# Layer two of a fourth batch in seven half-size products, squares and sums spread over three engines, and all pieces in a new order

## The chip, the core and the metric

The kernel runs on one NeuronCore of a Trainium2 chip. Five engines work side by side, each through its own list of instructions in a fixed order, and they wait for one another by semaphores: PE (TensorE) multiplies matrices into the accumulators of PSUM; DVE (VectorE), ACT (ScalarE) and POOL (GpSimd) do elementwise work; SP issues the stores. POOL also issues the loads of the inputs, as instructions in its own list, so that a load stands in line behind whatever POOL computes. The metric is the time of one execution on the device in microseconds (us). The kernel before took 225.02 us (median of three runs, 224.21 to 225.16).

## The reference

```python
scores = scale * np.matmul(x, state.transpose(0, 1, 3, 2))     # x: (8, 8, 512, 64), state: (8, 8, 32, 64)
a = softmax of scores over the 32 states;      xread = np.matmul(a, state)
scores2 = scale * np.matmul(state, x.transpose(0, 1, 3, 2))
a2 = softmax of scores2 over the 512 tokens;   sread = np.matmul(a2, x)
x = concatenate([xread, sread], axis=2), heads joined          # 8 batches x (512 + 32) rows x 512
h = x @ w_in                                                   # w_in: 512 x 2048
r = np.maximum(h, 0.0)
g = s * (r * r) + b
return g @ w_out                                               # w_out: 2048 x 512, out: 4352 x 512
```

(The softmaxes are shortened here.) Two cross attentions with 32 states to a head, and behind them a two-layer net whose activation is the squared rectifier.

## The kernel before

All inputs are cast to float16 on the way in; sums are float32. The eight batches run one behind the other in a pipeline, in the order 0 to 7, and the 256 rows of `sread` of all batches come last (`sr`).

The work is cut into pieces, each a small function, and the list `ORDER` names them one after the other: `name.argument.argument...`, where the letters A, V and G as an argument say ACT, DVE and POOL. The loop at the end of the kernel calls each piece in that order, so `ORDER` fixes the order of every engine's instructions; there is no other scheduler. The pieces that the text speaks of:

- Loads, all issued by POOL: `win.j` (a quarter of `w_in`), `wout.q` (a quarter of `w_out`), `x.b` and `xn.b` (a batch's `x` in two layouts), `st` (the states). Batch 0's `x` comes as float32 in four parts through SP's queue (`xf`) and is cast by `castx`. Eight loads of POOL can be under way; the ninth waits for the first to land. From batch 3 on `x.b` begins with a tiny copy (`ahead`) that waits for an earlier batch's transpose.
- First softmax: `xT` transposes `x` (DVE), `T` multiplies it with the states (PE), then `U`, `mu`, `D`, `E1`, `z`, `At`, `A`: transpose, maximum, subtraction, exponential (ACT), sum, scaling, transpose. For batch 0 they are done in two halves. `keep` copies `T` for later use. The second softmax is `nm`, `nms`, `E2`, `a2`, `aps`, `a2T`, `V`, `srd`.
- Layer one: since `xread` is `a` times the states, `M.b.j` first multiplies the states of a batch with quarter `j` of `w_in` (PE), `Mc` casts the result, and `l.b.f` multiplies it with `A` for feature block `f` of 16: two matmuls 128x512, then the rectifier on ACT into a tile `r` that holds four blocks. `lh` is the same for half of batch 0's tokens and two blocks at once. The sums of `l` have two buffers of PSUM (`hps`), so the matmuls of a third `l` wait for the rectifier of the first.
- `s.b.f.n.engine` squares `n` blocks of `r` into the tile `g` (`sh` for the halves of batch 0, `ssr` for the last rows).
- Layer two, plain: `L.b.rr.q`, four matmuls 128x512 for 128 tokens and a quarter of the 16 blocks; after four of them `out.b.rr` scales, adds the bias and stores.
- Layer two, with seven products for eight (Strassen's scheme in Winograd's form): for batches 5, 6 and 7 and the last rows. `wsum` makes four sums of the weights (`w_T1` to `w_T4`), `S.b.k.h.engine` four sums of quarters of `g` (half `h` of each), `P.b.u` half a product: eight matmuls 128x256. `ev` adds a finished product into the output tile `osx`, `put` stores it. `S_sr`, `P_sr`, `ev_sr` are the same for the last rows.
- `idle.n` multiplies ones by ones `n` times into a tile that nobody reads.

Work of several batches is woven together: while layer two of one batch runs on PE, softmax and layer one of the next go on, and the line breaks in `ORDER` stand where a batch's layer one begins.

Of the kernel before, what the change touches and what calls it, by code (L numbers as in the profile page):

```python
# [11 lines left out]
FP16 = mybir.dt.float16  # L12
# [3 lines left out]
    "win.0 win.1 wout.0 x.1 win.2 wout.1 win.3 wout.2 wout.3 idle.11 castx.1.0.V castx.0.0.A xT.0.0.0 "  # L16
    "casts.A turn.0.4.A pair.0.4 xT.0.1.0 T.0.1.0 U.0.0 mu.0.0 sb castx.1.1.A castx.0.1.A D.0.V.0 "
    "xT.0.0.1 idle.6 xT.0.1.1 E1.0.0 T.0.0.1 keep.0.0 M.0.0.1 Mc.0.0.A z.0.0 At.0.V.0 A.0.0 idle.4 "
    "M.0.1.1 Mc.0.1.A lh.0.0.0 U.0.1 mu.0.1 D.0.V.1 lh.0.2.0 keep.0.1 sh.0.0.0.V sh.0.2.0.V E1.0.1 z.0.1 "
    "At.0.V.1 L.0.1.0 lh.0.6.0 sh.0.6.0.G L.0.0.0 M.1.0.1 Mc.1.0.A lh.0.4.0 A.0.1 lh.0.6.1 xT.1.0 "  # L20
    "sh.0.4.0.G xT.1.1 T.1.1 U.1 lh.0.0.1 lh.0.4.1 lh.0.2.1 sh.0.2.1.G mu.1 M.0.2.0 Mc.0.2.A L.0.0.1 x.2 "
    "L.0.1.1 st D.1.V sh.0.6.1.V keep.1 l.0.9 l.0.8 M.0.3.1 Mc.0.3.V l.0.10 s.0.8.2.V cps.0 cps.1 E1.1 "
    "l.0.13 z.1 l.0.11 s.0.10.2.V At.1.V M.1.1.1 l.0.12 Mc.1.1.A l.0.14 l.0.15 L.0.0.2 s.0.12.2.A M.1.2.1 "
    "A.1 s.0.14.2.V Mc.1.2.A cps.2 cps.3 c L.0.1.2 l.1.1",
    "l.1.0 sh.0.0.1.V xT.2 M.1.3.1 x.3 L.0.0.3 bias out.0.0 l.1.2 Mc.1.3.V l.1.3 L.0.1.3 out.0.1 L.0.2.0 "
    "pair.4.16 sh.0.4.1.G turn.4.12.A L.0.2.1 l.1.4 turn.12.16.V T.2.1 keep.2 s.1.0.4.V l.1.5 l.1.6 "
    "L.0.2.2 l.1.8 U.2 mu.2 l.1.7 L.0.2.3 out.0.2 D.2.V l.1.9 s.1.8.2.V l.1.15 M.2.1.0 E1.2 z.2 M.2.0.1 "
# [24 lines left out]
    "L.4.3.0 L.4.3.1 l.5.11 xT.7 a2T.0.V s.5.8.4.V M.6.1.0 Mc.6.1.A A.6 M.6.2.1 out.4.2 l.5.13 l.5.12 "
    "s.5.12.2.V L.4.3.2 l.5.15 l.5.14 s.5.14.2.V L.4.3.3 P.5.0 out.4.3 Mc.6.2.A l.6.1 P.5.1 T.7.1 "
    "S.5.2.0.V S.5.3.1.V S.5.1.1.V V.6.0 srd.6 U.7 P.5.2 l.6.2 ev.5.X1 S.5.2.1.V",
    "l.6.0 keep.7 P.5.3 l.6.3 mu.7 S.5.4.0.V l.6.5 P.5.4 l.6.7 ev.5.Y srd.0 l.6.4 P.5.5 P.5.6 D.7.V E1.7 "
    "l.6.8 S.5.4.1.V P.5.7 l.6.6 M.6.3.0 s.6.0.4.V M.7.0.1 ev.5.X2 z.7 l.6.9 P.5.8 ev.5.W1 P.5.10 At.7.V "
    "Mc.7.0.A Mc.6.3.A s.6.4.2.V l.6.10 xn.7 P.5.9 s.6.6.2.V A.7 l.6.12 ev.5.X3 M.7.1.0 Mc.7.1.V M.7.2.1 "
    "nm.7 l.6.13 P.5.11 l.6.11 ev.5.W2 put.5.0.0 put.5.0.1 l.6.14 P.5.12 l.7.2 s.6.8.4.V S.6.3.0.V "
    "S.6.1.0.V P.5.13 Mc.7.2.A l.6.15 ev.5.X4",
    "l.7.0 s.6.14.2.V s.6.12.2.V S.6.3.1.V M.7.3.1 P.6.0 l.7.1 Mc.7.3.A l.7.6 P.6.1 put.5.1.0 nms.7.V "  # L60
    "E2.7.0 P.6.2 ev.6.X1 S.6.2.0.V S.6.1.1.V S.6.2.1.V put.5.1.1 l.7.12 l.7.3 E2.7.1 s.7.0.4.V P.6.3 "
    "a2.7 P.6.4 P.6.5 l.7.11 l.7.5 ev.6.Y aps.7 l.7.4 a2T.7.V S.6.4.0.V nm.1 nms.1.V P.6.6 l.7.8 ev.6.X2 "
    "l.7.15 V.7 srd.7 l.7.7 P.6.7 E2.1.1 E2.1.0 xn.1 P.6.8 P.6.9 ev.6.W1 a2.1 l.7.10 l.7.9 s.7.8.4.A "
    "S.6.4.1.V aps.1 s.7.4.4.V a2T.1.V ev.6.X3 P.6.10 P.6.11 ev.6.W2 put.6.0.0 put.6.0.1 l.7.14 "
    "s.7.14.2.V V.1 srd.1 S.7.3.0.V l.7.13 P.6.12 s.7.12.2.V P.6.13 P.7.0 lsr.6 S.7.1.0.V ev.6.X4 "
    "put.6.1.0 lsr.1 P.7.1 S.7.3.1.V S.7.2.0.V lsr.5 P.7.2 S.7.4.0.V P.7.3 lsr.2 lsr.3 ev.7.X1 P.7.4 "
    "ev.7.Y",
    "lsr.0 S.7.1.1.V S.7.2.1.V P.7.6 P.7.5 ssr.0.2.V lsr.9 ev.7.X2 ssr.2.2.V lsr.7 P.7.7 ev.7.W1 "
    "put.6.1.1 S.7.4.1.V lsr.8 ssr.8.2.V P.7.8 ssr.6.2.V lsr.4 ssr.4.2.V S_sr.3.0.V S_sr.1.0.V lsr.14 "
# [9 lines left out]
def kernel(  # L79
# [369 lines left out]
    def layer1(tag, f, terms, ntok):  # L449
# [4 lines left out]
        if (tag, q) not in R_t:  # L454
            R_t[tag, q] = rpool.tile([P, 4, ntok], FP16, name=f"r_{tag}_{q}", tag="r")
# [95 lines left out]
    def block(b, i, j):  # L551

        return G_t[b][:, j::2, HALF * i : HALF * i + HALF]
# [193 lines left out]
```

## Time and profile before

The profiled execution took 224.36 us, of which 222.2 us are the span from the first to the last instruction; 2.2 us lie around it. The median of the three runs is 0.66 us above the profiled execution.

| engine | busy us | share of the span | instructions |
|---|---|---|---|
| PE, matmuls | 210.7 | 95% | 1816 |
| DVE | 183.6 | 83% | 267 |
| ACT | 141.8 | 64% | 243 |
| POOL | 43.4 | 20% | 73 |

A busy PE says only that a matmul is in flight: matmuls are pipelined, and one of 128x512 shows 379 ns while the next starts 216 ns after it. What PE can do is read from the distance of the starts. Idle time of an engine that isn't the bound costs nothing by itself.

### The profile page before, as it was taken

How to read it: one execution, taken by the hardware profiler on the slowest of the kernel's cores; microseconds unless marked ns; L12 is line 12 of the kernel's file. 1: busy time of each engine (PE TensorE's matmuls, PEld its weight loads, DVE VectorE, ACT ScalarE, POOL GpSimd, SP SyncE). 2: the span in 40 equal slices, each digit the busy share in tenths (PEclk: the TensorE clock that was granted, in tenths of full speed). 3: DMA queues.
4: the chain of work that ended last, by engine and by line, in shares of the span. 5: the costliest groups of instructions: out<-in, count | busy, mean ns of one | idle time of the engine just before them, and what ended most of it. 6: DMA issues, size and time to landing. Idle time of an engine off the chain costs nothing.

```text
span 222.2 us, 4473 instructions
## 1 busy us (share of the span) xinstructions
PE 210.7 (95%) x1816; PEld 115.8 (52%) x1816; DVE 183.6 (83%) x267; ACT 141.8 (64%) x243; POOL 43.4 (20%) x73
## 2 busy tenths in 40 slices
PE   6469999999999999999999999999999999999992
PEld 2234334444444443444454544457766778888881
DVE  1597998889769997989796799889999997966772
ACT  2475895776488869855787479485877858533400
POOL 8245504000273400046002160005200000000000
PEclk9999999999999999999999999999999999999999
DMA  6999993420557892048927397226903500440066
GB/s 158 227 207 206 205 193 58 101 72 20 100 112 117 112 174 50 16 100 120 192 47 133 96 128 124 49 45 101 141 2 65 127 0 3 94 99 0 3 134 149
DMA packets 23416, 22.67 MB, mean 102 GB/s; under 512 B 4196, under 2 KB 16996, under 8 KB 23396
## 3 DMA queue, kind: packets, MB, share of 16 engines
q0 software_dynamic: 16560, 12.26, 38.6%
q1 hardware_dynamic: 6160, 9.97, 18.2%
q8 instruction: 14, 0.23, 0.4%
q10 hardware_dynamic: 676, 0.16, 0.3%
q14 instruction: 6, 0.05, 0.1%
HBM read 25.72 MB, written 8.91 MB: 156 GB/s over the span
## 4 chain that ended last, share of the span: by engine, by line
PE 88%; DMA 4%; DVE 3%; ACT 3%; SPq 1%; issue 0%
PE ops L496 31%; PE hps L452 24%; PE opf_X L137 9%; PE opf_W L137 5%; PE mps L137 4%; DMA xf<-in_x_dram 4%; PE hps_sr L452 3%; PE opf_Y L137 2%; PE vps L137 2%; PE T_None L137 2%; PE aps L137 2%; PE ops_sr_X L137 2%; ACT M L152 1%; DVE xT L289 1%; PE ops_sr_W L137 1%; ACT rh L482 1%
## 5 line engine op out<-in xcount | busy, mean ns | idle before, releaser
L456 ACT ACTIVATE r<-hps 128x512 f16<-128x512 f32 x120 | 69.3, 610 | 29.8 <-PE hps L452 28.4
L496 PE MATMUL ops<-w_out,g 128*128 128x512 f16 x320 | 78.1, 379 | 1.3 <-DVE g L462 1.3
L452 PE MATMUL hps<-A,M 128*128 128x512 f16 x240 | 65.3, 380 | 0.5 <-DVE M L152 0.3
L496 PEld LDWEIGHTS <-g 128*128 128x128 f16 x320 | 30.3, 98 | 38.4 <-issue 2.8
L462 DVE TENSOR_TENSOR g<-r 128x1024 f16<-128x1024 f16 (+1 forms) x39 | 34.5, 897 | 8.1 <-ACT r L456 8.0
L452 PEld LDWEIGHTS <-M 128*128 128x128 f16 x240 | 21.9, 98 | 25.8 <-issue 4.7
L137 PEld LDWEIGHTS <-g 128*128 128x128 f16 x288 | 28.0, 98 | 6.4 <-issue 0.2
L152 ACT CAST M<-mps 128x1024 f16<-128x1024 f32 x28 | 28.0, 1013 | 1.8 <-PE mps L137 1.8
L192 POOL DMA_DIRECT2D xn<-in_x_dram x32 | 18.5, 588 | 29.2 <-PE vps L137 28.3
L506 DVE SCALAR_TENSOR_TENSOR osb<-ops,sb_bc,bias_bc 128x512 f32<-128x512 f32 x20 | 14.7, 734 | 1.0 <-PE ops L496 1.0
L180 POOL COPY ahead<-xT 1x2 f16<-1x2 f16 x5 | 1.8, 367 | 67.0 <-DVE xT L289 67.0
L456 ACT ACTIVATE r_sr<-hps_sr 128x256 f16<-128x256 f32 x16 | 6.2, 385 | 12.8 <-PE hps_sr L452 12.4
L564 DVE TENSOR_TENSOR g<-g 128x1024 f16<-128x1024 f16 x18 | 12.2, 685 | 2.0 <-PE opf_Y L137 1.9
L289 DVE STREAM_TRANSPOSE xT<-xh 128x1024 f32<-128x1024 f32 (+2 forms) x12 | 10.3, 871 | 3.2 <-ACT xh L152 3.2
L333 DVE TENSOR_REDUCE z<-E 128x32 f32<-128x1024 f16 (+1 forms) x9 | 9.9, 1095 | 3.7 <-ACT E L328 3.7
L137 PE MATMUL opf_X<-w_T,g 128*128 128x256 f16 x96 | 11.9, 273 | 0.0
L137 PE MATMUL mps<-w_in,stT 64*32 64x512 f16 x256 | 11.2, 383 | 0.2 <-ACT M L152 0.2
L318 DVE TENSOR_REDUCE mu<-U 128x32 f32<-128x1024 f32 (+1 forms) x9 | 9.9, 1097 | 0.2
L376 ACT ACTIVATE E<-T_None,nms 128x512 f16<-128x512 f32 x8 | 5.5, 691 | 6.9 <-DVE nms L372 4.4
L328 ACT ACTIVATE E<-Dm 128x1024 f16<-128x1024 f32 (+1 forms) x9 | 8.7, 963 | 1.8 <-DVE Dm L322 1.5
L322 DVE TENSOR_TENSOR Dm<-U,mu 128x1024 f32<-128x1024 f32 (+1 forms) x8 | 9.6, 1201 | 0.2
L314 DVE STREAM_TRANSPOSE U<-T_None 128x1024 f32<-128x1024 f32 x7 | 8.7, 1247 | 1.2 <-PE T_None L137 0.8
(94 smaller groups left out, 259.4 us busy)
## 6 DMA issues: line engine op xcount, KB each, us to landing
out_dram<-osb SPq DMA_DIRECT2D x32, 128.0 KB, 2.7
xn<-in_x_dram POOLq DMA_DIRECT2D x32, 128.0 KB, 5.7
xh<-in_x_dram POOLq DMA_DIRECT2D x14, 256.0 KB, 5.2
out_dram<-osx SPq DMA_DIRECT2D x24, 128.0 KB, 2.4
w_in<-in_moe_w_in_dram POOLq DMA_DIRECT2D x8, 256.0 KB, 10.6
w_out<-in_moe_w_out_dram POOLq DMA_DIRECT2D x4, 512.0 KB, 12.7
xf<-in_x_dram SPq DMA_DIRECT2D x4, 256.0 KB, 7.5
out_dram<-osb SPq DMA_DIRECT2D x4, 256.0 KB
```

The costliest lines, as they stand in the source:

```text
L137: return nc.tensor.matmul(out, lhsT, rhs, start=start, stop=stop, tile_position=tp, is_transpose=is_transpose, skip_group_check=skip,)
L152: (engine.copy if engine is nc.scalar else engine.tensor_copy)(out, in_)
L192: nc.gpsimd.dma_start(out=xn_t[b][32 * jh : 32 * jh + 32].rearrange("t h c d -> t h (c d)"), in_=x[b].rearrange("h (t jh c) d -> jh t h (c ...
L289: nc.vector.transpose(part(out, p, g), part(in_, p, g))
L318: nc.vector.tensor_reduce(part(mu, p), blk(part(at[b]["U"], p)), AX.X, ALU.max)
L333: nc.vector.tensor_reduce(part(z, p), blk(part(at[b]["E1"], p)), AX.X, ALU.add)
L452: nc.tensor.matmul(hps, lhsT, rhs, start=(i == 0), stop=(i == len(terms) - 1))
L456: nc.scalar.activation(R_t[tag, q][:, i], hps, AF.Relu)
L462: e.tensor_mul(g, r, r)
L496: nc.tensor.matmul(ops_t[tag, rr], G_t[tag][:, f, P * rr : P * rr + P], w_out_f(f), start=(f == 0), stop=(f == NKF - 1),)
L506: nc.vector.scalar_tensor_tensor(osb, ops_t.pop((tag, rr)), s_bc, bias_bc, ALU.mult, ALU.add)
L564: e.tensor_tensor(out, x, y, op)
```

## The change

Batch 4 joins the batches whose layer two is done in seven products: its 16 pieces `L` and 4 pieces `out` go, and 14 `P`, 4 sums `S` in five pieces and 7 `ev`, 4 `put` come. Squares, sums, subtractions (`D`), scalings (`At`), casts (`Mc`) and copies are dealt anew to DVE, ACT and POOL; sums can now be made in one piece instead of two halves (the 2 in the place of `h`). The tiles of `r` are taken in turn from three buffers with names of their own instead of from one pool of three (four for the halves). And `ORDER` is new throughout; of 21 idle matmuls three are left.

Pieces by engine, before and after:

| piece | before | after |
|---|---|---|
| squares `s` of two blocks | 23 DVE, 1 ACT | 11 DVE, 14 ACT, 13 POOL |
| squares `s` of four blocks | 16 DVE, 2 ACT | 9 DVE, 2 ACT |
| squares `sh` | 4 DVE, 4 POOL | 4 DVE, 4 POOL |
| squares `ssr` | 8 DVE | 3 DVE, 5 ACT |
| `S`, half | 24 DVE | 17 DVE, 7 POOL |
| `S`, whole | none | 3 DVE, 1 POOL |
| `S_sr` | 8 halves DVE | 4 halves DVE, 2 halves and 1 whole POOL |
| `wsum` | 8 halves DVE | 2 halves and 1 whole DVE, 2 halves and 1 whole POOL |
| `D`, full batch | 6 DVE, 1 POOL | 3 DVE, 4 POOL |
| `At`, full batch | 7 DVE | 4 DVE, 3 POOL |
| `Mc` | 4 DVE, 28 ACT | 11 DVE, 21 ACT |
| `a2T` | 4 DVE, 4 ACT | 1 DVE, 7 ACT |
| `nms` | 6 DVE, 2 ACT | 2 DVE, 6 ACT |
| `castx`, `casts` | 1 DVE, 4 ACT | 3 DVE, 2 ACT |
| `L` and `out` | 80 and 20 | 64 and 16 |
| `P`, `ev`, `put` | 42, 21, 12 | 56, 28, 16 |
| matmuls of `idle` | 21 | 3 |

```diff
-    "win.0 win.1 wout.0 x.1 win.2 wout.1 win.3 wout.2 wout.3 idle.11 castx.1.0.V castx.0.0.A xT.0.0.0 "
-    "casts.A turn.0.4.A pair.0.4 xT.0.1.0 T.0.1.0 U.0.0 mu.0.0 sb castx.1.1.A castx.0.1.A D.0.V.0 "
-    "xT.0.0.1 idle.6 xT.0.1.1 E1.0.0 T.0.0.1 keep.0.0 M.0.0.1 Mc.0.0.A z.0.0 At.0.V.0 A.0.0 idle.4 "
-    "M.0.1.1 Mc.0.1.A lh.0.0.0 U.0.1 mu.0.1 D.0.V.1 lh.0.2.0 keep.0.1 sh.0.0.0.V sh.0.2.0.V E1.0.1 z.0.1 "
...
+    "castx.1.0.V castx.0.0.A win.0 xT.0.1.0 casts.V idle.1 idle.1 turn.0.4.A pair.0.4 xT.0.0.0 T.0.1.0 "
+    "keep.0.0 win.1 win.2 U.0.0 mu.0.0 D.0.V.0 castx.1.1.A E1.0.0 M.0.0.1 z.0.0 castx.0.1.V xT.0.0.1 "
+    "xT.0.1.1 wout.0 sb x.1 Mc.0.0.A wout.1 T.0.0.1 At.0.V.0 A.0.0 keep.0.1 M.0.1.1 Mc.0.1.A lh.0.0.0 "
+    "M.1.0.0 U.0.1 mu.0.1 D.0.V.1 E1.0.1 lh.0.6.0 lh.0.2.0 Mc.1.0.V sh.0.0.0.V M.0.2.0 win.3 sh.0.6.0.G "
+    "z.0.1 sh.0.2.0.V At.0.V.1 A.0.1 Mc.0.2.A idle.1 lh.0.4.0 M.1.1.1 M.1.2.0 sh.0.4.0.V Mc.1.1.A L.0.0.0 "
+    "wout.2 l.0.8 st l.0.9 s.0.8.2.G xT.1.0 l.0.11 xT.1.1 T.1.1 keep.1 U.1 mu.1 lh.0.6.1 sh.0.6.1.G D.1.V "
+    "lh.0.4.1 Mc.1.2.A L.0.1.0 lh.0.2.1 lh.0.0.1 sh.0.0.1.G L.0.1.1 E1.1 M.0.3.0 Mc.0.3.V M.1.3.1 l.0.10 "
+    "s.0.10.2.A L.0.0.1 Mc.1.3.A l.0.14 z.1 l.0.15 L.0.1.2 wout.3 At.1.V L.0.0.2 pair.4.16 turn.4.12.V "
+    "A.1 l.0.12 sh.0.4.1.G l.0.13 cps.0 cps.1 s.0.12.2.A cps.2 cps.3 s.0.14.2.V c sh.0.2.1.V l.1.3 x.2 "
...
+    "P.5.9 At.7.G ev.5.X3 Mc.7.1.A l.6.9 put.4.1.0 P.5.10 l.6.5 P.5.11 ev.5.W2 nms.1.A E2.1.1 l.6.15 A.7 "
+    "l.6.13 P.5.12 s.6.12.2.V s.6.4.2.G P.5.13 put.4.1.1 P.6.0 put.5.0.0 s.6.8.2.A s.6.14.2.V S.6.3.0.V "
+    "S.6.3.1.V l.7.6 l.7.12 ev.5.X4 xn.7 S.6.1.2.V aps.7 P.6.1 a2T.7.V",
+    "l.7.0 l.7.15 P.6.2 l.7.7 l.7.5 V.7 srd.7 l.7.14 P.6.3 ev.6.X1 l.7.4 E2.1.0 l.7.3 S.6.2.2.G P.6.4 "
...
+    turns = {}
+
+    def in_turn(shape, name, tag, n):
+        k = turns[tag] = turns.get(tag, -1) + 1
+        return rpool.tile(shape, FP16, name=name, tag=f"{tag}{k % n}", bufs=1)
+
     def layer1(tag, f, terms, ntok):
...
-            R_t[tag, q] = rpool.tile([P, 4, ntok], FP16, name=f"r_{tag}_{q}", tag="r")
+            R_t[tag, q] = in_turn([P, 4, ntok], f"r_{tag}_{q}", "r", 3)
...
-        r = R_t[b, f, p] = rpool.tile([P, 2, HALF], FP16, name=f"rh_{b}_{f}_{p}", tag="rh", bufs=4)
+        r = R_t[b, f, p] = in_turn([P, 2, HALF], f"rh_{b}_{f}_{p}", "rh", 4)
...
+    HALVES = (slice(0, 4), slice(4, 8), slice(0, 8))
...
-        A = lambda i, j: block(b, i, j)[:, 4 * h : 4 * h + 4]
+        sl = HALVES[h]
+        A = lambda i, j: block(b, i, j)[:, sl]
...
-        out, x, y = (t[:, 4 * h : 4 * h + 4] for t in (S_sr(name), x, y))
+        out, x, y = (t[:, HALVES[h]] for t in (S_sr(name), x, y))
```

`weight_sum` takes its slices from `HALVES` in the same way.

## The prediction

> **What bounds the kernel now.** I read the table of stages first (busy time of each engine in stretches of the span), then the timeline, then the groups by form, then the page's rows of the DMA engines.
>
> ```profile
> core 0: us, PE busy (x) PEld busy (x) DVE busy (x) ACT busy (x) POOL busy (x), PEclk, DMA share, GB/s
> 0.00:14.00 14.00, 8.89 (x73) 3.39 (x73) 7.03 (x15) 5.99 (x10) 7.86 (x16) 1.00 0.98 195
> 14.00:26.00 12.00, 10.19 (x91) 5.14 (x84) 10.59 (x15) 9.11 (x14) 5.47 (x7) 1.00 1.22 206
> ...
> 40.00:80.00 40.00, 40.00 (x278) 16.96 (x277) 34.66 (x45) 28.81 (x47) 10.05 (x15) 1.00 0.50 92
> ...
> 160.00:200.00 40.00, 40.00 (x404) 29.64 (x403) 34.97 (x55) 25.49 (x46) 0.00 (x0) 1.00 0.28 58
> ```
>
> PE is busy without a hole from 40 us on. Whether it is really full, the starts tell:
>
> ```profile
> 59.26 1.46 PE L496 MATMUL ops<-w_out,g 128*128 128x512 f16 x6
> 60.55 0.59 PE L452 MATMUL hps<-A,M 128*128 128x512 f16 x2
> 60.98 1.24 PE L496 MATMUL ops<-w_out,g 128*128 128x512 f16 x5
> ```
>
> ```profile
> 153.29 1.03 PE L452 MATMUL hps<-A,M 128*128 128x512 f16 x4
> 154.15 1.04 PE L137 MATMUL opf_Y<-w_out,g 128*128 128x256 f16 x8
> 155.03 1.03 PE L452 MATMUL hps<-A,M 128*128 128x512 f16 x4
> ```
>
> Two matmuls 128x512 take 0.43 us from start to start (60.55 to 60.98), four 0.86 (153.29 to 154.15), eight of 128x256 0.88 (154.15 to 155.03; 0.87 where no other form precedes). All pieces of a kind keep these distances from 40 us to the end. So with `L` at 0.863, `l` 0.432, `P` 0.873, `lh` and `lsr` 0.436, `M` 0.43, and the small rest the same way, matmul work is 203.8 us, and the last matmul ends at 218.1. What PE loses lies at the start: by 37.12 us, when two late `L` of batch 0 begin, 21.3 us of work are done, so 15.9 us are lost, 12.0 of them before the first `lh` at 14.16. Behind the last matmul stand 4.0 us of eviction and store, the same in both kernels.
>
> **Part by part.**
>
> *The product.* 16 `L` at 0.863 are 13.8 us, 14 `P` at 0.873 are 12.2. All of it lies on PE, the path: -1.6 us. Nothing else in PE's work changes but the idle matmuls: the first eleven (1.46 to 5.2 us) and the next ten stand in holes where PE waits anyway (the transposed `xT` at 11.5, `Mc` at 13.7), so taking them out gives nothing by itself.
>
> *The engines.* By the means of the groups, DVE sheds squares (7 of 1.21 us, 12 of 0.68, 5 of 0.42), 3 `D` of 1.2, 3 `At` of 1.29, 7 half sums of 0.69, `S_sr`, `wsum`, `a2T`, `nms` and 4 evictions of 0.73, together 45 us, and takes 7 casts of 1.21, 7 evictions of 0.74, four whole sums of 1.21 and two small casts, 19 to 20: from 183.6 to about 159 us. ACT takes 13 squares of 1.08, 5 `ssr` (0.55 each, half of that row), 3 `a2T` of 1.02, and sheds 7 casts of 1.01: 142 to about 154. POOL: nearest rows are the 128x512 square of 1.06 us and the 128x1024 `D` of 1.91. That is 1.9 to 2.1 us for 1024 elements and about 4.1 for 2048; 13 squares, 7 halves and one whole `S`, 4 pieces' worth of `wsum`, 4 `D`, 3 `At`, `S_sr` and the four `sh` make 77 us, where it was 6. With its loads POOL stands at about 114 us. None of the three comes near PE's 202, so by sums PE stays the bound. In the loads of 4 us stretches along the new order one is over: ACT has about 6 us against 3.5 of PE's around `V.6.0`, `E1.7` and `s.6.2.2.A`; four `P` follow there, which need no rectifier. I take 0 for it; without that cover it costs up to 2.
>
> *What runs against POOL.* The trace has it twice:
>
> ```profile
> 24.16 1.04 POOL L462 TENSOR_TENSOR g<-rh 128x512 f16<-128x512 f16 x1 [2.24 <-ACT rh L482]
> 24.17 2.11 DVE L322 TENSOR_TENSOR Dm<-U,mu 128x1024 f32<-128x1024 f32 x1
> ...
> 70.36 1.27 DVE L343 TENSOR_TENSOR At<-E,rz 128x1024 f16<-128x1024 f16 x1
> 70.50 1.14 POOL L180 COPY ahead<-xT 1x2 f16<-1x2 f16 x1 [4.02 <-DVE xT L289]
> ```
>
> The `D` that starts with POOL's square takes 2.11 us where the other five average 1.22: it waits until POOL is done. POOL's tiny copy, 0.17 us otherwise, starts under DVE's `At` and ends with it at 71.63. DVE's transposes and reductions beside POOL's squares show no such wait (0.67 and 0.71 at 19 to 20 us). So an operation of DVE that reads two tensors of SBUF and an operation of POOL exclude each other. The Trainium skill says so too (SBUF — State Buffer, section "SBUF: two separate sides"): the pair of ports is locked for a whole instruction and the loser blocks fully; the trace agrees with 1.04 against 0.89 us of delay. In the new kernel some 65 such DVE operations stand against 71 us of POOL's new work in 205: a third begin while POOL works and lose half an operation, 1.1 us, about 25 us in all. DVE is then at 184, as full as now, and PE was packed with that. How much reaches PE is bounded below by 0 and above by the places with little room. Squares on POOL are mostly due 5 to 26 us of PE's work after their rectifier. The tightest chain: `l.6.5`, `s.6.4.2.G`, the four loads `xn.7`, `S.6.2.2.G`, `P.6.4`. From the end of `l.6.5` to `P.6.4` PE has 11.9 us of other work; rectifier 0.9, square 2.1, four loads of 0.59 and the whole sum 4.1 make 9.5. 2.4 are spare; behind the square, `P.6.0` has 0.5, and at the end `P_sr.5` behind `S_sr.4.2.G` 0.7. I take +0.3, ends 0 and +3.
>
> *The start.* Here the order of loads decides: 204 to 206 GB/s are moved without a pause until 33 us, so 512 KB take 2.5 us. POOL's waits give the landings now: `w_in` quarter 0 at 10.9, quarter 1 at 13.1, `w_out` quarter 0 at 15.6, and on at that pace. In the new order `w_in` quarter 2 lands at 15.6, `w_out` 0 at 18.1, `x.1` at 20.6, `w_out` 1 at 23.1, `w_in` 3 at 25.6, `w_out` 2 at 28.1. `w_out` 3 stands in POOL's list behind the squares `s.0.8.2.G`, `sh.0.6.1.G` and `sh.0.0.1.G`; the last is done near 28, so it lands near 33, where it landed near 31. PE's loss must be at least landing minus work done before: 13.6 for `M.0.3`, 13.1 for `L.0.1.2`, 14.6 for `cps.3`. The softmax chain of batch 0 gives the same: `E1.0.0` no longer stands behind the cast of the last `xf` (10.36), so `A.0.0` ends at 13.6 instead of 14.1, but `M.0.1` still waits for 13.1. `lh.0.0.0` starts at 13.6 to 13.9, and following DVE's list by the same rows `A.0.1` ends at 20.0 and `T.1.1` starts at 21.9, with 7.8 us of work done: 14.0 lost, where it was 13.8. Later the rectifiers cost some 0.7 now and may again. Bounds for the loss: 14.6 and 16.2 against 15.9. I take -0.1, the middle leaning up for the clock:
>
> ```profile
> 1.46 3.88 PE L660 MATMUL dps<-ones 128*128 128x512 f16 x11 [1.46 <-DVE ones L221]
> ...
> 3.14 0.15 PEld L660 LDWEIGHTS <-ones 128*128 128x128 f16 x1 [0.28 <-issue]
> 3.57 0.15 PEld L660 LDWEIGHTS <-ones 128*128 128x128 f16 x1 [0.28 <-issue]
> 4.00 0.15 PEld L660 LDWEIGHTS <-ones 128*128 128x128 f16 x1 [0.28 <-issue]
> ```
>
> The idle matmuls start 0.43 us apart until 4.2 us and 0.216 after: PE runs at half speed until 2.7 us of dense work have passed, though the rows give the clock as 1.00 throughout. The new kernel has two there, so PE will be slow until `M.0.1` and the `lh` make it dense, from 13.1 to some 16 to 19 us. Then `T`, `M` and three `lh` take twice as long; on the chain to `lh.0.4.0` that is about +0.8, half of which `w_out` 3 hides. The Trainium skill (TensorE: Matmul & The Clock Gate, section "Part 1: The HAM clock gate") asks for a busy window of about 3.4 us that doesn't start with the kernel; by it the full clock comes between 16.5 and 20 us, an estimate, and the sum would be 0.3 us higher.
>
> *The sum.* -1.6 (products) -0.1 (start) +0.3 (POOL) = -1.4. The profiled execution before is 224.36, so this one would be 223.0; on the median, 0.66 higher, 225.02 - 1.4 = 223.6 us.
>
> **Rivals.**
>
> 1. The start gains. If the clock is up early and `w_out` 3 is in time, the loss falls to 14.6: -1.3 instead of -0.1, and no wait on POOL: 222.1 to 222.5. For it: more work of layer one is ready before `w_out` is. Against: DVE's chain to `A.0.1` isn't shorter.
> 2. Slower: POOL's pace. If POOL's operations with their waits take twice the nearest rows (4.2 for 1024, 8.3 for 2048), the chain to `P.6.4` takes 15.8 instead of 9.5 against 11.9 of other work: PE waits 3.9 us, 1.6 of it already at `P.6.0`: 225.02 - 1.7 + 3.9 = 227.2. It is slower by over 0.5% from a delay of 2.8 us on, POOL at about 1.8 times the rows; at 1.5 times (1 to 1.5 us at PE) it is about even. For it: five operations of POOL with two inputs are all that the trace shows. Against: the four squares took 1.04 to 1.10.
> 3. Slower: the clock stays down. If PE stays slow until 26 us, the 12 us from 14 on yield half: 6 us less work, less some 2.5 of waiting that there is anyway: +3.5, so 226.8. For it: PE has about 2 us of work in the 12 us before. Against: now it stays up through a hole of 2.1 us (before the `T` at 11.51).
> 4. The work saved doesn't show: small waits at PE of 1.6 us in all eat it: 225.0.
>
> **How the numbers follow.** A measurement of this kernel can tell about 0.5% from no change, 1.1 us: faster is under 223.9, slower over 226.1. Chances: forecast 0.45 (its own range 222.9 to 224.6, 0.31 of it under 223.9), start gains 0.15, POOL's pace 0.18 (0.13 slower, 0.05 even), clock 0.10 slower, nothing shows 0.12 (0.03 slower). Faster 0.31 + 0.15 = 0.46, same 0.14 + 0.05 + 0.09 = 0.28, slower 0.13 + 0.10 + 0.03 = 0.26. The range reaches from the first rival's end, 222.0, to just under the prices of the second and third, 227.0.
>
> **What would show it.** Right: `P` and `L` still 0.87 and 0.86 apart from 40 us on; 112 more matmuls of `opf` and 64 fewer of `ops`; DVE near 160 plus what it is blocked; the last matmul some 4 us before the end. The start is read from the work done by 37 us. Wrong if PE shows holes behind 40 us that `S` or squares on POOL end (step of POOL), if a 128x1024 square on POOL is far from 2.1 us, or if `hph` starts stay 0.22 apart beyond 20 us (clock).

## The result and the profile after

The changed kernel takes 241.27 us (median of four, 240.07 to 241.38), the kernel before on the same chip 225.09 (four, 224.21 to 225.94). The ratio is 1.071, with a 95% interval of 1.065 to 1.076: some 16 us slower, where 223.6 was forecast and 222.0 to 227.0 was the range. The profiled execution took 240.07 us with a span of 238.3, against 222.2 before.

The page of the changed kernel, its first rows: busy time by engine, then PE and its granted clock in 40 slices of 6 us.

```profile
PE 209.8 (88%) x1846; PEld 121.2 (51%) x1846; DVE 177.6 (75%) x229; ACT 154.1 (65%) x259; POOL 112.6 (47%) x106
PE   1489989799937999999999995599999989999992
PEclk9999999999997999999999999799999999999998
```

The sums are near the forecast ones: ACT was put at 154 us, POOL at 114, DVE at 159 plus what it is held. The row of PE shows what isn't: two holes, at about 66 to 71 and 143 to 155 us, and a dip of the clock behind each. The table of stages says the same (the columns are as in the table before):

```profile
0.00:14.00 14.00, 4.92 (x54) 1.65 (x54) 7.44 (x17) 5.34 (x9) 7.97 (x16) 1.00 0.98 195
14.00:26.00 12.00, 11.57 (x105) 5.64 (x98) 9.68 (x16) 10.53 (x17) 5.85 (x5) 1.00 1.22 207
40.00:80.00 40.00, 32.88 (x236) 14.01 (x221) 34.17 (x31) 23.16 (x38) 27.87 (x26) 0.96 0.61 106
80.00:120.00 40.00, 40.00 (x341) 17.95 (x340) 31.75 (x41) 31.13 (x55) 17.47 (x17) 1.00 0.44 80
120.00:160.00 40.00, 34.70 (x295) 20.11 (x294) 34.68 (x37) 25.12 (x46) 18.00 (x17) 0.96 0.42 67
160.00:200.00 40.00, 38.91 (x418) 27.75 (x417) 28.95 (x43) 30.58 (x50) 18.87 (x14) 1.00 0.43 80
```

From 40 to 80 us PE stands idle for 7.1 of 40, where it had no hole before; from 120 to 160 for 5.3. In the first of these POOL works 27.9 us instead of 10.1. From 80 to 120 us PE has no hole, and in the first 40 us it is busy 3.4 us less than before, with 18 idle matmuls gone.

The timeline at the first hole. Each row is one instruction or group: start, length, engine, line, operation, tiles, and in brackets the idle time before it and what ended that.

```profile
61.79 3.82 DVE L386 TENSOR_SCALAR a<-E,q 128x512 f16<-128x512 f16 x1
63.26 2.14 POOL L543 TENSOR_TENSOR w_T<-w_out 128x1024 f16<-128x1024 f16 x1
65.53 3.83 DVE L386 TENSOR_SCALAR a<-E,q 128x512 f16<-128x512 f16 x1
67.32 1.88 POOL L469 TENSOR_TENSOR g<-r 128x1024 f16<-128x1024 f16 x1
71.88 0.69 ACT L377 ACTIVATE E<-T_None,nms 128x512 f16<-128x512 f32 x1 [6.00 <-DVE U L315]
73.19 1.01 PE L459 MATMUL hps<-A,M 128*128 128x512 f16 x2 [5.47 <-ACT r L463]
```

The two scalings `a2.3` take 3.82 and 3.83 us; the same operation took 0.35 us in the kernel before, where the groups give the usual lengths of a scaling and of a square (busy time in all, then the mean in ns):

```profile
L385 DVE TENSOR_SCALAR a<-E,q 128x512 f16<-128x512 f16 x16 | 4.9, 350 | 0.4
L462 DVE TENSOR_TENSOR g<-r 128x1024 f16<-128x1024 f16 x23 | 15.2, 677 | 6.0 <-ACT r L456 6.0
```

The first scaling ends with POOL's half sum `wsum.T3.0.G` (63.26 to 65.40), the second with the two squares `s.2.0.2.G` and `s.2.2.2.G` behind it (65.35 to 69.20). Behind the scalings DVE has `nm.4` and `U.4`; ACT stands 6.00 us at `E2.4`, which by the profile waits for `U.4` (both read the same sums), and behind `E2.4` stand the rectifiers that PE waits 5.47 us for. The second hole:

```profile
143.27 2.34 POOL L193 DMA_DIRECT2D xn<-in_x_dram  x4
143.80 6.44 DVE L469 TENSOR_TENSOR g<-r 128x1024 f16<-128x1024 f16 x1
145.62 4.06 POOL L543 TENSOR_TENSOR w_T<-w_out,w_T 128x2048 f16<-128x2048 f16 x1
150.94 0.60 ACT L463 ACTIVATE r<-hps 128x512 f16<-128x512 f32 x1 [5.53 <-DVE g L469]
151.58 1.01 PE L459 MATMUL hps<-A,M 128*128 128x512 f16 x2 [5.30 <-ACT r L463]
```

A square of 0.68 us takes 6.44 and ends 0.56 us after POOL's whole sum `wsum.T4.2.G`. It holds the tile `r` that the next rectifier wants. These three instructions make 12.7 of the 13.9 us by which DVE's operations exceed their usual lengths in the whole kernel.

The clock, in stretches around the first hole (the number behind that of POOL is the granted clock):

```profile
68.00:72.60 4.60, 0.00 (x0) 0.00 (x0) 4.53 (x5) 0.72 (x3) 3.52 (x5) 1.00 0.65 84
72.60:76.00 3.40, 2.81 (x13) 1.55 (x13) 3.37 (x6) 2.53 (x5) 0.00 (x0) 0.50 0.86 134
76.00:80.00 4.00, 4.00 (x20) 1.79 (x19) 1.03 (x1) 0.70 (x2) 1.92 (x1) 1.00 0.39 84
```

After 5 us without a matmul the clock stands at one half for 3.4 us, and again from 151.1 to 154.5. PE works 2.8 and 2.9 us of these two stretches at half speed and so loses another 1.4 us each. The Trainium skill says so (TensorE: Matmul & The Clock Gate, section "Part 1: The HAM clock gate": an idle window of about 3.4 us halves the clock); the trace agrees, with 3.41 us in its records of the clock. Other runs here don't agree in full: the clock also halved behind a wait of 2.27 us and stayed up behind one of 3.40 (see the experiments).

So of the 16.1 us of span, 5.5 + 5.3 are the two waits and 2.9 the clock behind them. Small waits that weren't there before make most of the rest: 0.97 and 0.51 at `M.2.1.1` and `M.2.0.0`, 0.7 at `cps.3`, 0.4 at `M.6.3.0`, 0.7 at `V.7`. Against them stand the 1.6 us of matmul work saved.

### The profile page after: what moved, and what is told of

Same layout as the page of the kernel before. It is cut to its first block, busy times and chain, and to the rows that moved or that the text cites. A ratio compares the mean times of both kernels' runs of the same rounds, so it can differ in the third digit from the quotient of the medians.

```text
span 238.3 us, 4559 instructions
## 1 busy us (share of the span) xinstructions
PE 209.8 (88%) x1846; PEld 121.2 (51%) x1846; DVE 177.6 (75%) x229; ACT 154.1 (65%) x259; POOL 112.6 (47%) x106
## 4 chain that ended last, share of the span: by engine, by line
PE 68%; DVE 13%; DMA 7%; ACT 5%; issue 3%; POOL 2%; ACTq 0%; POOLq 0%; DVEq 0%
PE ops L503 19%; PE hps L459 17%; PE opf_X L138 10%; PE opf_W L138 6%; DVE a L386 3%; PE hps_sr L459 3%; DVE g L469 3%; PE mps L138 3%; DMA xh<-in_x_dram 3%; PE opf_Y L138 3%; DMA xn<-in_x_dram 2%; DMA ident<-ident_const 2%; PE vps L138 2%; PE hph L138 2%; PE aps L138 2%
## 5 line engine op out<-in xcount | busy, mean ns | idle before, releaser
L503 PE MATMUL ops<-w_out,g 128*128 128x512 f16 x256 | 63.0, 382 | 0.1
L469 POOL TENSOR_TENSOR g<-r 128x1024 f16<-128x1024 f16 x13 | 24.6, 1905 | 24.6 <-PE ops L503 15.6
L573 POOL TENSOR_TENSOR g<-g 128x1024 f16<-128x1024 f16 (+1 forms) x6 | 15.0, 2502 | 31.2 <-DVE g L573 22.9
L469 DVE TENSOR_TENSOR g<-r 128x1024 f16<-128x1024 f16 (+1 forms) x20 | 23.9, 1209 | 3.4 <-ACT r L463 3.1
L467 ACT ACTIVATE g<-r 128x1024 f16<-128x1024 f16 (+1 forms) x16 | 18.7, 1178 | 0.3
L153 DVE CAST M<-mps 128x1024 f16<-128x1024 f32 x11 | 13.3, 1220 | 3.9 <-PE mps L138 3.8
L138 PE MATMUL opf_X<-w_T,g 128*128 128x256 f16 x128 | 16.1, 273 | 0.0
L602 DVE SCALAR_TENSOR_TENSOR osx<-opf_X,sb_bc,bias_bc 128x512 f32<-128x512 f32 x12 | 8.9, 746 | 7.8 <-PE opf_X L138 6.7
L323 POOL TENSOR_TENSOR Dm<-U,mu 128x1024 f32<-128x1024 f32 x4 | 7.6, 1910 | 10.5 <-DVE mu L319 10.5
L386 DVE TENSOR_SCALAR a<-E,q 128x512 f16<-128x512 f16 x16 | 12.2, 806 | 0.3
L573 DVE TENSOR_TENSOR g<-g 128x1024 f16<-128x1024 f16 (+1 forms) x15 | 11.4, 778 | 0.1
```

The source lines that it names most:

```text
L138: return nc.tensor.matmul(out, lhsT, rhs, start=start, stop=stop, tile_position=tp, is_transpose=is_transpose, skip_group_check=skip,)
L153: (engine.copy if engine is nc.scalar else engine.tensor_copy)(out, in_)
L386: nc.vector.tensor_scalar(a2[:, g].rearrange("p (c jh t) -> p jh c t", c=4, jh=4), at[b]["E2"][:, g].rearrange("p (jh c t) -> p jh c t", c ...
L467: nc.scalar.activation(g, r, AF.Square)
L469: e.tensor_mul(g, r, r)
L503: nc.tensor.matmul(ops_t[tag, rr], G_t[tag][:, f, P * rr : P * rr + P], w_out_f(f), start=(f == 0), stop=(f == NKF - 1),)
```

## The experiments

Three theories were tried first. *Train*: when loads and a ready operation stand one behind the other in POOL's list, they keep DVE out from some point in the loads to the operation's end. *Single lock*: only POOL's operation itself keeps DVE out, for its own length. *Not POOL*: the three long rows have another cause.

**The two weight sums back on DVE.**

```diff
- wsum.T3.0.G ... wsum.T4.2.G
+ wsum.T3.0.V ... wsum.T4.2.V
```

> Two sums of the weights (the first half of T3, the whole of T4) go from POOL back to DVE, nothing else; DVE gets about 1.8 us more work. Theory 'train': an operation of POOL whose inputs are ready, but which stands behind loads in POOL's list, keeps DVE's two-tensor operations and fast scalings out while the loads are still being issued, and then for its own time. Then the square of 6.44 us at 143.8 takes 0.68 again, PE's wait of 5.3 us behind it and the half clock after that wait (3.4 us, 1.4 lost) go; of the two scalings of 3.8 us at 61.8 one stays held, by the two squares that stand behind the same loads: 2 of 5.5 us go. In all -8 to -9 from 241.3: 232 to 233.5 us. Theory 'single lock' (POOL keeps DVE out only while its operation itself runs): -4 for T4 and -2 for T3: 235 us. Theory 'not POOL' (those operations of DVE wait for something else): 241 to 243 us, the long operations stay.

Measured: 229.78 us, ratio 1.024 (1.021 to 1.027). Two letters take back 11.5 of the 16 us, more than any theory gave. Both holes are gone; as the sums weren't moved one by one, the 11.5 us aren't divided between them. The list of PE's waits (total, times, longest), of the changed kernel and then of this one:

```profile
PE hps L459 <- ACT r L463: 11.0, 3, 5.5
```

```profile
PE opf_X L138 <- DVE w_T L543: 2.3, 1, 2.3
PE hps L459 <- ACT r L463: 0.9, 2, 0.6
```

The second scaling, which two squares of POOL had held, is free too: it now runs at 62.56, ahead of the squares. So the sums started the chain. The new 2.3 us are of the experiment's making: `T4` stands late in DVE's list and `P.4.12` waits for it.

**The two squares to DVE as well.**

```diff
- s.2.0.2.G s.2.2.2.G
+ s.2.0.2.V s.2.2.2.V
```

> As the run before, and the two squares of batch 2's blocks 0 to 3 go to DVE as well, so that no POOL operation stands ready behind loads at either place. Train: both long holds go, with PE's waits (5.5 and 5.3 us) and the half clock behind them (1.4 us each): -13, so 227 to 229 us; PE's loss behind the first 40 us falls from 15 to about 2 us. Single lock: -4 for T4, -2 for T3, -3.8 for the squares: 231 to 232. Not POOL: 241 to 244 us.

Measured: 229.87 us, ratio 1.024 (1.020 to 1.027). Nothing is gained over the run before, and the time lies just above the 227 to 229 us that *train* gave. So these squares did harm only by standing behind the sum; moving them alone was not tried.

**One sum to POOL in the kernel before.**

```diff
- l.2.12 wsum.T1.1.V l.2.11
+ l.2.12 l.2.11
- xn.4 E2.4.0
+ xn.4 wsum.T1.1.G E2.4.0
```

> The kernel before with one half sum of the weights (T1, second half, 0.68 us on DVE) made by POOL and put right behind the six loads that POOL issues at 71.6 to 75. DVE has less work, POOL one operation of 2.1 us more. Train: a two-tensor operation of DVE that comes while those loads are issued (72 to 75 us) is held until the sum is done at about 77: one operation of 4 to 5 us, PE waits 2 to 4 us there, 227 to 229 us. Single lock: no operation of DVE is longer than 0.7 + 2.1 us, and only one that starts while the sum runs: 225 to 226 us. Not POOL: 225 us, no long operation.

Measured: 228.58 us, ratio 1.019 (1.013 to 1.025). One half sum, moved behind six loads of POOL, costs 4.3 us in a kernel that has nothing else of the change, as *train* gave (227 to 229):

```profile
74.12 4.75 DVE L462 TENSOR_TENSOR g<-r 128x2048 f16<-128x2048 f16 x1
75.61 2.16 POOL L535 TENSOR_TENSOR w_T<-w_out 128x1024 f16<-128x1024 f16 x1
79.61 1.86 PE L452 MATMUL hps<-A,M 128*128 128x512 f16 x4 [2.27 <-ACT r L456]
```

The square is held from its start, 1.5 us ahead of the sum's, through the last four loads (73.28 to 75.63) and the sum; its own 1.2 us follow. PE waits 2.27 us and then runs 3.4 us at half clock (the start had another such stretch in this execution, from 11.1 to 14.5 us). *Single lock* explains 2.2 of the 3.5 us of holding, not the rest.

**Two probes of the cost by itself.** The first lets DVE and POOL start side by side, with the computation left out and zeros written: products 128x1024 or scalings 128x512 on DVE, loads and products on POOL.

> A probe that leaves the whole computation out and writes zeros. In each phase DVE and POOL are let go together by ACT. DVE does eight products 128x1024 (0.6 us apart), fourteen scalings 128x512 (0.27) or five transposes; POOL does, by phase: 0 nothing; 1 four loads; 2 four loads and a ready product 128x2048; 3 the same, but the product's input comes from ACT about 6 us later; 4 three products 128x1024 in a row; 5 a product 128x2048 and then four loads; 6 scalings against four loads and a ready product; 7 transposes against the same; 8 as 2; 9 scalings against loads alone; 10 scalings against three products. Train: in 2, 6 and 8 one operation of DVE takes 5 to 6.5 us (rest of the loads' 2.3 plus 4.1), in 3 one takes at most 4.8, in 1, 7 and 9 none is longer than alone; in 4 and 10 one is held for two or three products on end (4 to 6 us). Single lock: 4.1 + 0.7 at most in 2, 3, 5, 6, 8, and 2.1 + 0.7 at most in 4 and 10. If loads alone hold DVE: 1 and 9 show it too.

Loads alone held nothing: 677 ns a product of DVE beside four loads, 683 without. Loads ahead of a product whose input came late held nothing either; that product itself ran only when DVE's row was over, so its own effect isn't seen there. A ready product did hold DVE, with the scaling's hold beginning 1.7 us ahead of it (first pair); and where POOL had three products on end, two-input products of DVE got a turn between them (2.6 us each), a scaling got none until all three were done (second pair; the row of POOL is the second of the three, which run from 90.90 to 97.16):

```profile
63.29 5.92 DVE L72 TENSOR_SCALAR ov<-a 128x512 f16<-128x512 f16 x1
64.98 4.07 POOL L102 TENSOR_TENSOR op<-pa,pb 128x2048 f16<-128x2048 f16 x1
...
90.40 6.92 DVE L72 TENSOR_SCALAR ov<-a 128x512 f16<-128x512 f16 x1
92.98 2.11 POOL L102 TENSOR_TENSOR op<-pa,pb 128x1024 f16<-128x1024 f16 x1
```

The second probe measures the lead with shorter instructions.

> The whole computation is left out and zeros are written: products 128x512 of DVE (some 0.35 us each, then scalings of the same size) in a row beside POOL, which issues 0, 1, 2, 3 or 4 loads and then does a ready product 128x1024 (2 us; with 3 loads 128x2048). Theory that POOL takes DVE's way to SBUF as soon as its product stands next, while the loads before it are still being worked off: the held instruction of DVE starts ahead of the product's own start by up to 0.4 us with no load and by 0.5 to 1.8 us with loads, and lasts product plus that. Rival, that the lead is the length of the whole train of loads: 0.6, 1.2 and 2.3 us with 1, 2 and 4 loads. Rival, that the lead is only the time by which the one instruction of DVE that happens to be under way overlaps the product: up to 0.4 us in every phase. A tiny copy 1x2 in the product's place: by the first theory one instruction held 0.5 to 1.8 us, by the third none over 0.6.

The held instruction of DVE and POOL's operation with no load ahead, one load, and four; then a tiny copy behind four loads:

```profile
16.57 2.21 POOL L102 TENSOR_TENSOR op<-pa,pb 128x1024 f16<-128x1024 f16 x1
16.74 2.33 DVE L127 TENSOR_TENSOR ov<-a,b 128x512 f16<-128x512 f16 x1
...
21.33 2.94 DVE L127 TENSOR_TENSOR ov<-a,b 128x512 f16<-128x512 f16 x1
21.86 2.13 POOL L102 TENSOR_TENSOR op<-pa,pb 128x1024 f16<-128x1024 f16 x1
...
39.42 3.25 DVE L127 TENSOR_TENSOR ov<-a,b 128x512 f16<-128x512 f16 x1
40.26 2.13 POOL L102 TENSOR_TENSOR op<-pa,pb 128x1024 f16<-128x1024 f16 x1
...
84.36 4.44 DVE L127 TENSOR_TENSOR ov<-a,b 128x512 f16<-128x512 f16 x13
84.74 4.10 POOL L143 COPY tiny<-pa 1x2 f16<-1x2 f16 x1
```

With no load there is no lead: DVE's instruction starts after POOL's. With one load it is held from 0.52 us ahead, with three 0.63, with four 0.83; a scaling is held from 0.56 us ahead with two loads and from 0.53 with four. So the rival falls by which the lead is the whole train (2.3 us for four loads), and the one by which it is only the overlap of the instruction under way (up to 0.4 us). The kernels show up to 1.8 us, the first probe up to 1.7; what sets it between 0.5 and 1.8 stays open. The last pair was not foreseen: the exclusion goes both ways. DVE's row of products let POOL's copy of 0.17 us wait 4.1 us, until the row was done; a POOL product took 5.5 and 4.4 us in two other phases for the same reason. And once a single load of POOL took 3.05 us instead of 0.6, through a whole row of scalings; in the other phases with scalings loads took 0.58 to 0.69, beside two-input products 0.58 to 0.76. The Trainium skill has the case (SBUF — State Buffer, section "SBUF: two separate sides": an operation of DVE that takes both ports keeps POOL from writing descriptors), and the 3.05 us agree, though only in that one phase.

**The loads behind the sum, no engine changed.**

```diff
- l.5.12 xn.6 T.7.1
+ l.5.12 T.7.1
- wsum.T4.2.G S.5.3.0.V
+ wsum.T4.2.G xn.6 S.5.3.0.V
```

> The changed kernel with one thing of the order moved and no engine changed: the four loads xn.6 stand behind the whole weight sum T4 in POOL's list, not ahead of it. Theory that POOL's sum, ready and queued behind loads, holds DVE from the loads on: the sum now starts at once near 143.4 and ends near 147.4, so the square s.5.4 that starts near 143.8 is held about 4.3 us instead of 6.44 and PE waits about 3.2 instead of 5.30; 237.5 to 239.3 us. Rival, that DVE is held only while the sum itself runs and the loads play no part: the hold is 4.3 as well, but then the hold of 6.44 in the changed kernel is not explained. Rival, that loads and sum hold DVE as one train whatever their order: the hold stays at 6.4 and the time at 241.

Measured: 237.46 us, ratio 1.057 (1.051 to 1.062), 3.8 less than the changed kernel and at the lower end of the theory's range.

```profile
142.86 4.51 POOL L543 TENSOR_TENSOR w_T<-w_out,w_T 128x2048 f16<-128x2048 f16 x1
143.37 4.54 DVE L469 TENSOR_TENSOR g<-r 128x1024 f16<-128x1024 f16 x1
147.32 4.62 POOL L193 DMA_DIRECT2D xn<-in_x_dram  x8
149.26 0.59 PE L459 MATMUL hps<-A,M 128*128 128x512 f16 x2 [3.40 <-ACT r L463]
```

The hold is 4.54 instead of 6.44 us and the wait 3.40 instead of 5.30. The 1.9 us between are what the loads ahead of the sum had added; the order in POOL's list alone does it. Behind the shorter wait the clock stayed up in this execution, which is another 1.4 us.

**What else is lost.** With sums and squares on DVE 4 to 5 us against the kernel before are left. On top of that kernel four single places were mended, and then idle matmuls added:

```diff
- xT.2 x.3 l.1.5 bias L.0.1.3 l.1.7 out.0.1
+ l.1.5 bias L.0.1.3 out.0.1 xT.2 x.3 l.1.7
- z.6 Mc.5.3.A
+ z.6 wsum.T4.2.V Mc.5.3.A
- S.5.4.1.G P.5.4 ... xn.7 S.6.1.2.V
+ S.5.4.1.G xn.7 P.5.4 ... S.6.1.2.V
- M.6.3.0 Mc.6.3.A ... P.5.6
+ P.5.6 M.6.3.0 Mc.6.3.A ...
```

> The changed kernel with the two whole weight sums T3 and T4 and the squares s.2.0 and s.2.2 on DVE, and four places of the order mended that still lost time in the run with both sums and squares moved (229.87 us, profiled 228.58): bias and out.0.1 ahead of xT.2 on DVE (M.2.1.1 and M.2.0.0 had lost 1.13 + 0.48, L.0.2.0 0.45), T4 earlier on DVE (P.4.12 had lost 2.47, the experiment's own loss), the loads xn.7 earlier on POOL (V.7 had lost 1.0), P.5.6 ahead of M.6.3.0 (0.59). Theory that the new kernel's loss was POOL holding DVE plus these few waits, and that the products are worth their 1.6 us: 228.6 less 5.0 to 6.1 is 222.5 to 223.6 for an execution at full clock, median 222.5 to 224.3. Rival, that the new order is short of slack everywhere and each wait mended is taken over by one behind it: 226 to 229. Rival, that the 16 L of batch 4 were no dearer than the 14 P in effect: all waits gone and still 224.3 or more.

> The run with the waits mended, and 14 idle matmuls more at the start (11 instead of 2 ahead of the first real one, 5 ahead of the second group). Theory that the start with few idle matmuls leaves the clock near its edge (clock 0.989 to 0.991 in three of four executions of the run with sums and squares on DVE, these 1.3 us slower than the fourth at 0.999): 0.5 to 1.3 us below the run without them. Rival, that the start costs nothing: within 0.3 us of it. Rival, that the idle matmuls stand in the way of the first real ones: 0.3 to 1 us above it.

The first missed: the profiled execution took 227.41 us at clock 1.00, five more 230.9 to 231.9 at 0.985 to 0.993. The second tells nothing: with the idle matmuls the median was 230.33 (ratio 1.024, 1.019 to 1.029), 1.0 us below the median without them, but the profiled execution, 228.84, was 1.4 us above its counterpart. The waits aimed at were gone or smaller, and a new one stood in front, for a transpose whose `x.3` had come late:

```profile
46.08 0.41 PE L138 MATMUL mps<-w_in,stT 64*32 64x512 f16 x8
49.35 0.64 PE L138 MATMUL T_None<-xT,stE 32*32 32x512 f16 x16 [2.86 <-DVE xT L290]
```

POOL issued `x.3` at the same time as in the run before (39.2), but its transpose could start only at 48.05 instead of 45.89; a store now comes ahead of the load, and that this is what delayed it was not shown apart. With the idle matmuls PE was 0.3 us earlier at `T.2.1`, the same wait of 2.85 us came, and this time the clock halved behind it (eight matmuls of `L.0.3` took 3.5 us). The traces show what decides. In their records the clock changes only at whole steps of 3.41 us, counted from its first rise, and what goes ahead of a halving is a step in which PE was busy for a small share, not a wait of a certain length. With the idle matmuls the wait of 2.85 us lay within one step (46.78 to 50.19), of which PE was busy for 0.33; without them the wait of 2.86 us lay across two, busy for 0.57 and 0.60. In the kernel before with one sum on POOL a share of 0.41 (75.93 to 79.35) halved the clock after a wait of only 2.27 us; with the loads behind the sum it stayed up at 0.43 (147.33 to 150.74), after a wait of 3.40. Over all profiled executions of the kernels a step with a share of 0.41 or less was always followed by the half clock and one with 0.51 or more never; between these, both came. What makes the 3 to 4 us between the profiled execution and the five others was not shown: a halved step costs at most 1.7 us.

The next pair issued `x.3` right behind `x.2` and put four sums `S` on DVE:

```diff
- x.2 ... xT.2 x.3
+ x.2 x.3 ... xT.2
- S.4.2.0.G S.4.4.0.G S.5.4.0.G S.5.4.1.G
+ S.4.2.0.V S.4.4.0.V S.5.4.0.V S.5.4.1.V
```

> The run with the waits mended, with its own new loss and three small ones mended too: the loads x.3 issued right behind x.2 (the tiny copy ahead of them left out for this one batch; T.3.1 had waited 2.86 us for the transpose of a late x.3), M.2.0.0 behind l.1.6 (0.5), the sums S.4.2.0, S.4.4.0, S.5.4.0, S.5.4.1 on DVE and S.5.2.1 earlier (0.43 at P.4.4, 0.35 at P.5.5). Theory that the wait for x.3 also cost the other executions their clock (0.985 to 0.993 where the profiled one had 1.0): 227.4 less 3.9 to 4.3 is 223.1 to 223.5 at full clock, the median 223 to 225. Rival, that the clock is lost elsewhere, at the start: median 226 to 228 with the profiled one 2 us or more below it or above it by chance. Rival, that the earlier loads collide with w_out and x.2: a new wait at cps or T.2.1, 225 to 228.

> The same with 14 idle matmuls more at the start (11 and 5 as before). In the last pair the start itself was 0.3 us earlier with them. Theory that the clock was lost at the wait for x.3 alone: 0.1 to 0.4 us below the run without. Theory that it is lost at the start in executions that the profile does not show: 1 to 2 us below. Rival, that the idle matmuls bring the next loss of the clock on: 0.5 to 2 us above.

Measured: 226.91 (ratio 1.009, 1.006 to 1.013) and 227.22 (1.010, 1.007 to 1.013); neither theory held, and the idle matmuls gain nothing. With them PE has its full clock from 6.6 us on instead of 18.9, but loses it again from 13.5 to 16.9, when the first `lh` run. And the mended waits were taken over again: `l.1.6` waited 1.0 us for a rectifier where `M.2.0.0` had waited 0.5, and with all four sums on DVE `P.4.4` waited 1.6 us for them. The wait of 0.77 us at `cps.3` is not due to the earlier `x.3`: it was 0.69 in the changed kernel, and 0.83 in the next run, where `x.3` comes late again. Here POOL's share did help: with `S.4.2.0` and `S.4.4.0` on POOL that place had lost at most 0.4.

The next one went back to what moves no load or store forward:

```diff
- bias L.0.1.3 ... out.0.0 ... U.2
+ bias xT.2 x.3 L.0.1.3 ... U.2 out.0.0
- s.5.4.2.V l.5.7
+ s.5.4.2.V wsum.T4.2.V l.5.7
```

> The changed kernel with T3, T4, s.2.0 and s.2.2 on DVE, and only such waits mended as moved no load or store forward at the start: bias ahead of xT.2 and U.2 ahead of out.0.0 on DVE, T4 behind s.5.4 (POOL's two sums S.4.2.0 and S.4.4.0 stay on POOL), xn.7 earlier, S.5.4.0 on DVE, S.5.2.1 and P.5.6 earlier. Against the run with both sums and squares moved (profiled 228.58): T4 no longer waited for, -2.5; M.2.1.1 and L.0.2.0, -1.0 to -1.5; V.7, -1.0; M.6.3.0, -0.5: 223.1 to 223.6 at full clock. Theory that only single waits are left: median 223 to 224.7, at or below the kernel before (224.7). Rival, that each mended wait is taken over by the next (as in the two runs before): 225 to 227.

Measured: 226.00, ratio 1.005 (1.002 to 1.007), better than the runs before it, but in the rival's range. What is left of the start is `w_out` 3: POOL issues it at 28.58, behind three squares, and PE waits for it. Then only the order of loads was changed:

```diff
- st l.0.9 ... L.0.1.2 wout.3 At.1.V ... l.1.3 x.2
+ st wout.3 l.0.9 ... sh.0.0.1.G x.2 L.0.1.1 ... L.0.1.2 At.1.V ... l.1.3
```

> The run with the least moved (226.0 us, profiled 225.90), with two loads earlier in POOL's list: w_out 3 right behind the states' load (POOL issues it near 20.3 us instead of 28.6, where it stands behind three squares) and x.2 behind the square sh.0.0.1 (near 28 instead of 30.4). PE waits 0.77 us for w_out 3 at cps.3 there and has lost 16.1 us by then against 15.7 in the kernel before. Theory that the order of POOL's loads is what the start still loses: cps.3 waits no longer, M.2.1.1 comes 0.8 to 1.2 us earlier, 224.7 to 225.2 us, the same as the kernel before. Rival, that loads and computations of the start are bound by something else (the casts, the rectifiers): within 0.3 us of 226.0. Rival, that loads ahead of ready squares hold DVE: 226.3 or more.

Measured: 224.92, ratio 1.000 (0.998 to 1.002), as expected. POOL's issue of `w_out` 3 and PE's sums over it, first without and then with the load earlier:

```profile
28.58 0.81 POOL L207 DMA_DIRECT2D w_out<-in_moe_w_out_dram  x1
34.59 0.40 PE L138 MATMUL cps<-w_out,ones 128*32 128x512 f16 x4 [0.83 <-DMA w_out<-in_moe_w_out_dram]
```

```profile
20.22 0.76 POOL L207 DMA_DIRECT2D w_out<-in_moe_w_out_dram  x1
32.65 1.05 PE L138 MATMUL cps<-w_out,ones 128*32 128x512 f16 x16
```

The last one mended what still stood over 0.2 us at PE behind 40 us:

```diff
- s.5.4.2.V wsum.T4.2.V l.5.7 s.5.6.2.V
+ s.5.4.2.V l.5.7 s.5.6.2.V wsum.T4.2.V
- S.5.4.1.G
+ S.5.4.1.V
- M.2.1.1 Mc.2.1.A M.2.0.0 l.1.6 Mc.2.0.V L.0.3.0 L.0.3.1 xT.3 E1.2 l.1.15 M.2.3.0
+ L.0.3.0 M.2.1.1 Mc.2.1.A L.0.3.1 l.1.6 xT.3 l.1.15 M.2.0.0 Mc.2.0.V E1.2 L.0.3.2 M.2.3.0
```

> The run with two loads earlier (224.92 us, profiled 224.62), and its last waits at PE mended by order and by one engine: T4 behind s.5.6 (l.5.13 waits 0.75 for a rectifier whose tile the square behind T4 frees), S.5.4.1 on DVE (it holds the square s.6.6 to 2.25 us; P.5.8 0.52 and l.6.14 0.25), M.2.1.1 behind L.0.3.0 and M.2.0.0 behind l.1.15 (0.54 and 0.49). Theory that the products do save their 1.6 us and only these waits cover it: 224.9 less 1.5 to 2.0 is 222.9 to 223.4, ratio 0.990 to 0.994. Rival, that a wait mended is taken over by the next (as in two runs): 224.3 to 225.2, and then the saving can't be had with this order.

Measured: 224.30, ratio 0.997 (0.995 to 0.9995): 0.65 us below the kernel before, just told from it, and 0.6 below the run before where theory gave 1.5 to 2.0; it is the rival's range. New small waits (0.7 at `M.2.3.0`, 0.4 at `P.4.8`) took over a part. So the new kernel, mended, keeps some of the products' 1.6 us; that all of it can be had was not shown.

## Why the prediction was wrong, step by step

*What runs against POOL* is the step that failed. It had the mechanism right, that certain operations of DVE and any operation of POOL exclude each other, and priced it wrongly in three ways. The sum had +0.3 us for it, at most 3; the two waits at PE measured 10.8 us and the half clock behind them 2.9. It took half an operation of POOL, 1.1 us, for each of a third of 65 operations, spread evenly: 25 us in all, of which 0 to 3 at PE. In the trace only seven operations ran over by more than 0.06 us, by 13.9 us in all, but 12.7 of them in three instructions, 3.5 to 5.8 us each. First, what holds is the longest thing that POOL has at that place, the sums of 2.1 and 4.1 us and runs of several operations, not half of a mean one. Secondly, a ready operation behind loads holds 0.5 to 1.8 us longer than it lasts, which the traces before could not show, having no such pair. Thirdly, scalings were left out of the 65: they read one tensor, and the trace before had no row for one beside POOL's work. They are held too, and through several operations of POOL on end.

*The places with little room* were looked for on the wrong side. The step followed what POOL computes (`l.6.5`, `s.6.4.2.G`, `xn.7`, `S.6.2.2.G`, `P.6.4`) and found 2.4 us to spare; `P.6.4` indeed saw no wait, and only `V.7` lost 0.7 us behind `xn.7`. What went late is what DVE was kept from: a scaling, with `nm`, `U`, then ACT's `E2` and the rectifiers in line behind it, and a square whose tile the next rectifier needs. There is little room in these chains: holding of 5.76 us in the second gave a wait of 5.30 at PE and 3.86 with the loads behind gave 3.40, 0.46 less in both; 6.95 in the first gave 5.47, and 3.54 in the kernel before 2.27.

*The clock* was counted only at the start. Each wait of over 5 us at PE cost 1.4 us more.

*The product*: right as work. PE's work is 1.6 us less than the 203.8 before, and `L` and `P` keep their distances: four matmuls of `L` and of `l` stand 0.86 us apart (63.24, 64.10, 64.96), and `hps_sr` and `opf` stand 0.87 and 0.88 apart in the changed kernel:

```profile
208.57 1.04 PE L459 MATMUL hps_sr<-srdT,w_in 128*128 128x256 f16 x8
209.44 1.04 PE L138 MATMUL opf_X<-w_out,g 128*128 128x256 f16 x8
210.32 1.04 PE L138 MATMUL opf_Y<-w_out,g 128*128 128x256 f16 x8
```

*The start*: predicted -0.1 with bounds of 14.6 and 16.2 on the loss. In the changed kernel 16.3 us are lost when `L.0.0.3` begins at 37.85, against 15.9 before: +0.4, just over the upper bound, so rival 1 is out. The full clock came at 18.0 us, within the forecast 16 to 19, so rival 3 is out too. `w_out` 3 let PE go on at 34.7 instead of near 33, for the reason named there, POOL's squares ahead of it, and moving it ahead of them, together with `x.2`, gave 1.1 us.

*The engines*: the sizes on POOL were right (1.91 us for 1024 elements, 4.06 for 2048), so rival 2, POOL at twice the rows, is out; the sums of ACT and POOL were right within 2 us, and DVE's own work is 163.7 (177.6 less the 13.9 of holding) against 159. Part of that gap is arithmetic: the terms named for what DVE sheds add up to about 42 us, not 45. ACT's overload near `V.6.0`, taken as 0, cost 0.4 at `M.6.3.0`.

*The range* ended at 227.0, below even rival 2's own 227.2, which was priced as one wait of 3.9 us. Two longer ones came, and each brought the clock along. And rival 4, small waits that eat the work saved, is what remains once the holds are gone: from 229.9 down to 224.3 some ten such waits had to be mended one by one, and some came back elsewhere.

## What to carry to other kernels

Before work goes to POOL, list for every operation of POOL which two-input operations and scalings of DVE start in its time or in that of the loads ahead of it, and follow those, not POOL's result: what is held is the whole operation plus the loads' lead, and it costs what stands behind the victim on DVE, ACT and PE. A long operation of POOL that is ready while loads are issued ahead of it was the worst case here: putting one ahead of the loads gave 3.8 us, leaving two on DVE 11.5. Busy times by engine can be forecast to a few us and the time still be wrong by 18.

## What the runs showed of the hardware

- A ready POOL operation behind loads keeps DVE out from 0.5 to 1.8 us ahead of its own start; without loads there is no lead (a start 0.16 us after POOL's). Loads alone hold nothing (677 ns against 683).
- The exclusion goes both ways: DVE's uninterrupted row of thirteen products held POOL's copy of 0.17 us for 4.1 us.
- Two-input operations of DVE get a turn between two operations of POOL (2.6 us each); a scaling got none through three (6.92 us).
- One load of POOL took 3.05 us instead of 0.6 beside a row of scalings on DVE; in the other phases with scalings loads took 0.58 to 0.69.
- PE's clock changed only at steps of 3.41 us. It halved after waits of 5.5, 5.3, 2.85 and 2.27 us and stayed up after others of 3.40 and 2.86; a step in which PE was busy for 0.41 or less was always followed by the half clock, one with 0.51 or more never.
